# Strided and local attention with a Mish MLP: a new order of local k's transposes and of the strided P·V in the first batch

## The chip, the cores and the metric

The kernel runs on one core of a Trainium2 chip. The metric is the device time of one execution in microseconds (us), as the median of several runs. The engines of the core work side by side, each through its own queue in order: TensorE (PE; its weight loads are listed as PEld), VectorE (DVE), ScalarE (ACT), GpSimd (POOL) and SyncE (SP, here only a queue of DMAs). PE writes its results into PSUM, from where DVE and ACT copy them on.

## The reference, cut to what matters

There are 8 batches, 8 heads, 576 positions and a head dimension of 64. Heads 0 to 3 are local (a query sees the 32 positions up to its own), heads 4 to 7 are strided (a query sees earlier positions with the same remainder modulo 32). The attention's output feeds an MLP on 4608 tokens.

```
scores = scale * np.matmul(q, k.transpose(0, 1, 3, 2))
mask_local = (rel >= 0) & (rel < stride)
mask_strided = (rel >= 0) & (pos[None, :] % stride == pos[:, None] % stride)
scores = np.where(masks[None, :, :, :], scores, -1000000000.0)
attn = np.exp(scores - max); attn = attn / (sum(attn) + 1e-09)
x = matmul(attn, v) as [4608, 512]
h = x @ w_in                      # 512 -> 2048
g = h * np.tanh(softplus(h))      # Mish
out = g @ w_out                   # 2048 -> 512
```

## The kernel before, in words

The work runs in nine token blocks of 512 for the MLP (t = 0 to 8) and eight batches of attention. From batch 1 on, the attention of a batch is spread in small steps between the matmuls of the MLP. Batch 0 has nothing to be spread into: lines 693 to 740 are its attention by itself, written out by hand in the order in which each engine's queue gets it, and the edit is in there. There is no planner; what is emitted first on an engine is done first on it (`manual_schedule`, L649), and semaphores hold an instruction until its inputs are written and the memory that it writes is free.

The stages of batch 0, and the helpers that emit them:

- `t_step(b, kind, which, hp, eng)` (L221) transposes one half (two heads) of q or k on PE into a PSUM tile `tr`, 8 transposes for the strided kind "s" (L229) and 12 for the local kind "l" (L243), and copies it to SBUF on the engine that is named (L180 on ACT, L182 on DVE): `kTs`, `qTs`, `kTl`, `qTl`. The PSUM tiles come from a pool of two buffers (`tile_t`, L114), used in turn, so that the next but one can be written only when the copy out of the first is done.
- `a.bias(kind, i, i_acc)` (L274) writes the mask into one of three accumulators of two banks each (acc0, acc1, acc2), by matmuls of an identity with a constant (L280). `a.qk([(kind, i)], None, ps)` (L287) adds the scores on top (L303) and lets ACT take their exp into `P_s[i]` or `P_l[i]` (L311). Both kinds come in three parts: 12, 12 and 8 matmuls with 864, 864 and 576 columns for "s", and 10, 10 and 4 with 960, 960 and 384 for "l".
- `a.pv2(kind, i, i_acc)` (L350) does P·V for the pair i, i+1 in an accumulator (8 matmuls, L333); DVE then takes the reciprocal of the row sums (L358) and scales the result into `x_s` or `x_l` (L359). Strided pairs 0, 2, 4 and 6 need parts 0, 0 and 1, 1, and 2. Local pairs 0, 2 and 4 need parts 0, 0 and 1, and 1 and 2.
- `unread(n, i_acc)` (L253) issues n matmuls of 512 columns of zeros, whose result nobody reads. They go to a `tr` tile, or to an accumulator if one is named.
- `a.xt(kind, hf)` (L364) transposes the result (L372, L382) and ACT copies it into `xT`, the MLP's input. `mlp1(0, accs)` (L453) then multiplies by `w_in` (L473, 64 matmuls for t = 0) and ACT takes Mish (L483); `mlp2` multiplies by `w_out` (L573), with the attention of batch 1 between its steps.

The loads that matter here are emitted long ahead: `load_early_loc(0)` (L138) issues the local k and q of batch 0 on POOL's queue. `spread_v_str(0, Dv)` is a DVE copy of the strided v. `load_w_out`, `load_qk_str(1)` and the others of L723 to L730 follow behind the part that is changed.

An accumulator is free for its next use when the engine that reads it is done: ACT's exp for scores, DVE's scaling for P·V. In the old order, the three strided parts use acc0, acc1 and acc2, the strided pairs acc0, acc1, acc0, acc0, the local parts acc2, acc1, acc2, and the local pairs acc1, acc0, acc2.

Of the kernel before, what the change touches and what calls it, by code (L numbers as in the profile page):

```python
# [43 lines left out]
def kernel(ctx, tc, q, k, v, moe_w_in, moe_w_out, out):  # L44
# [55 lines left out]
    def acc(i, name):  # L100

        pool = ps_z[0] if i == 2 else ps_a
        return pool.tile([128, 2, 512], F32, tag=f"acc{i}", name=name)
# [10 lines left out]
    def tile_t(name):  # L114
        return ps_t.tile([128, 512], F32, tag="pt", name=name)
# [11 lines left out]
    def by_head(x):  # L127

        return x[0:PL].rearrange("p j h d -> p (j h d)").rearrange("p (h x) -> p h x", h=4)
# [19 lines left out]
    def spread_v_str(b, eng):  # L149
        cast(eng, vs[b % 2][0:PN, :, :, 0:D], vs_raw().rearrange("p h (j d) -> p h j d", d=D))  # L150
# [27 lines left out]
    def cast(eng, out_, in_):  # L178
        if eng is nc.scalar:
            nc.scalar.copy(out_, in_)  # L180
        else:
            eng.tensor_copy(out_, in_)  # L182
# [38 lines left out]
    def t_step(b, kind, which, hp, eng=None):  # L221

        eng = eng or nc.vector
        tr = tile_t("tr")[:].bitcast(BF16)
        if kind == "s":
            src = (qs if which == "q" else ks)[b % 2]
            for u in range(8):
                h, jj = 2 * hp + u // 4, u % 4
                nc.tensor.transpose(  # L229
                    tr[:, PN * u:PN * u + PN],  # L230
                    src[0:PN, h, 128 * jj:128 * jj + 128],
                    ident[0:PN, 0:PN],
                )
            dst = (qTs if which == "q" else kTs)[:, 8 * SU * hp:8 * SU * hp + 8 * SU]
            cast(
                eng, dst.rearrange("c (u n) -> c u n", u=8)[:, :, 0:PN],
                tr[:, 0:S].rearrange("c (u n) -> c u n", u=8),
            )
        else:
            src = by_head((ql if which == "q" else kl)[b % 2])  # L240
            for j in range(CL):
                for e in range(2):
                    nc.tensor.transpose(  # L243
                        tr[64 * e:64 * e + 64, PL * j:PL * j + PL],
                        src[:, 2 * hp + e, D * j:D * j + D], ident[0:PL, 0:PL],
                    )
            dst = qTl[:, hp, :] if which == "q" else kTl[:, hp, 32:32 + S]
            cast(
                eng, dst.rearrange("c (p j) -> c p j", j=CL),
                tr[:, 0:S].rearrange("c (j p) -> c p j", j=CL),  # L250
            )

    def unread(n, i_acc=None):  # L253

        tr = tile_t("un")[:] if i_acc is None else acc(i_acc, "un")[:, 0, :]
        for _ in range(n):
            nc.tensor.matmul(tr, lhsT=zeros[:, 0:128], rhs=zeros[:], start=True, stop=True)
# [391 lines left out]
    with tc.manual_schedule():  # L649
        Po, Dv, Sc = nc.gpsimd, nc.vector, nc.scalar  # L650
# [42 lines left out]
        a = Attn(0)  # L693
# [5 lines left out]
        ps = [a.bias("s", i, i) for i in range(2)]  # L699
# [2 lines left out]
        t_step(0, "s", "q", 1, Dv)  # L702
        unread(2, 2)
        ps.append(a.bias("s", 2, 2))
        for i in range(3):
            a.qk([("s", i)], None, ps[i])
        spread_v_str(0, Dv)
        unread(2)
        a.pv2("s", 0, 0)
        for hp in range(2):  # L710
            t_step(0, "l", "k", hp, Sc)
        a.pv2("s", 2, 1)
        unread(2, 2)
        t_step(0, "l", "q", 0, Sc)
        t_step(0, "l", "q", 1, Dv)
        ps = [a.bias("l", 0, 2)]
        a.pv2("s", 4, 0)
        ps.append(a.bias("l", 1, 1))
        a.qk([("l", 0)], None, ps[0])
        a.qk([("l", 1)], None, ps[1])  # L720
        a.pv2("s", 6, 0)
        a.qk([("l", 2)], None, a.bias("l", 2, 2))
        load_w_out(0, 1)  # L723
        load_qk_str(1)
# [117 lines left out]
```

## Time and profile before

| | us |
|---|---|
| median of 3 runs | 305.48 (305.15 to 305.68) |
| the profiled execution | 304.4 |
| its span, first to last instruction | 302.6 |
| PE busy in the span | 293.1 |
| first strided exp, end of the third | 12.25, 14.45 |
| transposes of local k, of local q (first one's start) | 13.54, 15.03 |
| first local exp, start | 17.53 |
| first local P·V, start | 19.42 |
| dense stretch of the first MLP product, start | 22.77 |
| first transposes of batch 1, start | 35.72 |

The profile is that of one execution; its times are in us from the start of its span. A line of the timeline has the start, the time until the end, engine, line, operation, output and inputs, the shape, how often, and in brackets how long the engine was idle before and what ended this. Matmuls are pipelined: one of 512 columns is shown as taking 0.38, but they follow each other every 0.21 to 0.22. A line of the chain of waits has a start, a length, and what was under way in the chain of work that ended last.

### The profile page before, as it was taken

Reading aid. Unit: us, or ns where it says so; the run is one execution under the profiler, and the core shown is the slowest. Engines: PE = TensorE matmul, PEld = TensorE weight load, DVE = VectorE, ACT = ScalarE, POOL = GpSimd, SP = SyncE. Lnnn points to the kernel's source line nnn. Section 1 sums busy time; section 2 is a strip of 40 time slices with the busy share of each in tenths; the row PEclk is TensorE's granted clock in tenths of the full one; section 3 lists DMA queues with packets and bytes.
Section 4 is the critical chain, followed back from the end, with each engine's and each line's share of the span. In section 5 each row is a group of like instructions: output and inputs, shape, how many; then the busy total and the mean of one; then the engine's idle time right before and its main releaser. Section 6 shows DMA issues by size and latency. Waiting matters only on the chain.

```text
span 302.6 us, 6850 instructions
## 1 busy us (share of the span) xinstructions
PE 293.1 (97%) x2900; PEld 197.9 (65%) x2922; DVE 155.8 (51%) x356; ACT 171.7 (57%) x220; POOL 105.4 (35%) x116
## 2 busy tenths in 40 slices
PE   8889999999999999999999999999999999999995
PEld 3554556546884588458889885478646864684484
DVE  2370166868660857086617662576348544620732
ACT  2568634677655765667456855685467636414620
POOL 8284402324491419240934085206620410000000
PEclk9999999999999999999999999999999999999999
DMA  8999999979999998999979975994590030003003
GB/s 158 186 202 194 194 195 191 187 133 200 242 162 188 284 164 129 117 277 174 114 121 281 169 98 100 280 143 84 67 255 1 3 141 0 2 0 141 0 0 141
DMA packets 103738, 43.25 MB, mean 143 GB/s; under 512 B 86172, under 2 KB 99212, under 8 KB 103708
## 3 DMA queue, kind: packets, MB, share of 16 engines
q1 hardware_dynamic: 86620, 30.05, 55.9%
q0 software_dynamic: 16800, 12.51, 27.9%
q8 instruction: 23, 0.38, 0.6%
q10 hardware_dynamic: 288, 0.25, 0.3%
q14 instruction: 7, 0.06, 0.1%
HBM read 38.38 MB, written 9.44 MB: 158 GB/s over the span
## 4 chain that ended last, share of the span: by engine, by line
PE 89%; DVE 3%; DMA 3%; ACT 2%; issue 1%; POOL 0%; ACTq 0%; POOLq 0%
PE psh L473 32%; PE pso L545 28%; PE psb L473 9%; PE po L333 4%; PE pso L573 4%; PE pso L600 4%; PE ps L303 4%; DMA qs<-in_q_dram 3%; DVE x_l L359 2%; PE trx L372 1%; PE trx L382 1%; ACT Ps L311 1%; DVE osb L524 1%; PE tr L229 1%; PE tr L243 1%
## 5 line engine op out<-in xcount | busy, mean ns | idle before, releaser
L473 PE MATMUL psh<-xT,w_in 128*128 128x512 bf16 (+1 forms) x484 | 100.7, 358 | 0.8
L473 PEld LDWEIGHTS <-w_in 128*128 128x128 bf16 x640 | 61.5, 98 | 58.2 <-issue 0.7
L483 ACT ACTIVATE gT<-psh 128x1024 bf16<-128x1024 f32 x56 | 56.3, 1023 | 45.5 <-PE psh L473 43.1
L497 DVE TENSOR_TENSOR Sg<-gT 128x256 bf16<-128x256 bf16 (+2 forms) x64 | 28.4, 450 | 51.0 <-ACT gT L483 48.9
L317 POOL TENSOR_TENSOR Pl<-Pl,consts_sb 128x960 bf16<-128x960 bf16 (+1 forms) x18 | 29.2, 1632 | 48.5 <-ACT Pl L311 48.5
L545 PEld LDWEIGHTS <-Sg 128*128 128x128 bf16 x448 | 41.9, 98 | 6.3
L545 PE MATMUL pso<-Tw,Sg 128*128 128x256 bf16 x336 | 40.1, 273 | 0.0
L545 PEld LDWEIGHTS <-gT 128*128 128x128 bf16 x336 | 31.3, 98 | 4.6
L182 POOL CAST vl<-vl 128x768 bf16<-128x768 f32 x15 | 13.6, 931 | 59.4 <-DMA vl<-in_v_dram 59.4
L180 ACT COPY xT<-trx 128x576 bf16<-128x576 bf16 x32 | 20.1, 639 | 20.0 <-PE trx L382 14.0
L473 PE MATMUL psb<-xT,w_in 128*128 128x512 bf16 (+1 forms) x141 | 30.1, 355 | 0.2
L180 ACT COPY osb<-pso 128x512 f32<-128x512 f32 (+1 forms) x26 | 14.1, 544 | 26.4 <-PE pso L545 16.1
L545 PE MATMUL pso<-w_out,gT 128*128 128x256 bf16 x224 | 27.8, 273 | 0.0
L311 ACT ACTIVATE Pl<-ps 128x960 bf16<-128x960 f32 (+1 forms) x24 | 19.2, 807 | 11.6 <-PE ps L303 11.4
L524 DVE TENSOR_TENSOR osb<-pso,osb 128x512 f32<-128x512 f32 x21 | 14.5, 692 | 21.4 <-PE pso L545 21.4
L311 ACT ACTIVATE Ps<-ps 72x864 bf16<-72x864 f32 (+1 forms) x24 | 18.5, 803 | 5.3 <-PE ps L303 5.1
L479 ACT ACTIVATE gT<-psb 128x512 bf16<-128x512 f32 x32 | 19.0, 598 | 2.9 <-PE psb L473 2.5
L359 DVE TENSOR_TENSOR x_s<-po,rden 72x512 bf16<-72x512 f32 x28 | 19.2, 686 | 1.0
L497 DVE TENSOR_TENSOR Sg<-Sg,gT 128x256 bf16<-128x256 bf16 (+2 forms) x32 | 16.2, 506 | 1.1
L573 PE MATMUL pso<-w_out,gT 128*128 128x512 bf16 x59 | 15.8, 380 | 0.5 <-issue 0.3
L333 PEld LDWEIGHTS <-Ps 72*128 72x128 bf16 x256 | 12.1, 97 | 5.4 <-DVE Ps L317 1.7
L344 DVE RECIPROCAL rden<-po 96x4 f32<-96x4 f32 (+1 forms) x22 | 3.9, 178 | 22.1 <-PE po L333 22.0
(90 smaller groups left out, 343.4 us busy)
## 6 DMA issues: line engine op xcount, KB each, us to landing
out_dram<-osb SPq DMA_DIRECT2D x16, 512.0 KB, 6.2
vl<-in_v_dram SPq DMA_DIRECT2D x7, 768.0 KB, 6.9
kl<-in_k_dram SPq DMA_DIRECT2D x6, 576.0 KB, 9.9
ql<-in_q_dram SPq DMA_DIRECT2D x6, 576.0 KB, 13.1
qs<-in_q_dram POOLq DMA_DIRECT2D x8, 288.0 KB, 11.0
vsr<-in_v_dram POOLq DMA_DIRECT2D x8, 288.0 KB, 7.4
w_in<-in_moe_w_in_dram POOLq DMA_DIRECT2D x4, 512.0 KB, 9.7
w_out<-in_moe_w_out_dram POOLq DMA_DIRECT2D x4, 512.0 KB, 17.3
```

Source lines behind the costliest of these rows:

```text
L180: nc.scalar.copy(out_, in_)
L311: nc.scalar.activation(pt[0:n, :, 0:nw], ps[0:n, :, o0:o0 + nw], AF.Exp, scale=scale)
L317: meng.tensor_tensor(out=pm, in0=pm, in1=mk[0:n, :].unsqueeze(1).unsqueeze(1).to_broadcast([n, 2, nu, w]), op=ALU.mult,)
L333: nc.tensor.matmul(po[:, h, :], lhsT=pt[0:n, c0:c0 + 128], rhs=rhs, start=True, stop=True,)
L359: nc.vector.tensor_tensor(out=dst.rearrange("p e (h d) -> p e h d", h=4), in0=po[0:m, :, :, 0:D], in1=rden[0:m].unsqueeze(3).to_broadcast( ...
L473: nc.tensor.matmul(ps_u[:, o:o + n], lhsT=w_in[:, cc, fc * 128:(fc + 1) * 128], rhs=xT[:, cc, a:a + n], start=(cc == 2 and (o == 0 or len( ...
L479: nc.scalar.activation(gT[:, g + 8 * u, :], ps_u[:], AF.Mish)
L483: nc.scalar.activation(to, tiles[g][:], AF.Mish)
L497: nc.vector.tensor_tensor(out=out_, in0=in0, in1=in1, op=op)
L524: add = lambda o, p: nc.vector.tensor_tensor(out=o, in0=p, in1=o, op=ALU.add)
L545: nc.tensor.matmul(ps[:, pair, :], lhsT=lhs(c, 128 * pair), rhs=rhs(c), start=(first and pair == 0 and c == 0), stop=(last and c == 7), sk ...
L573: nc.tensor.matmul(p[:, ot % 2, :], lhsT=gT[:, fc, 128 * ot:128 * ot + 128], rhs=w_out[:, fc, :], start=(fc == 0), stop=(fc == 15),)
```

## The change

The edit is in lines 705 to 721, all of it in the order of batch 0's attention.

The transposes of local k, which stood behind the first strided P·V, now stand ahead of the third strided scores. Half 0 is copied by DVE instead of ACT; half 1 stays on ACT, where its copy is now between the second and the third strided exp. Three fillers stand ahead of them instead of two, and the two fillers ahead of local q are gone. The first two strided P·V pairs follow the third strided scores. Both halves of local q are copied by ACT; half 1 was copied by DVE.

The fourth strided P·V pair (pair 6) is moved ahead of the local scores, and goes from acc0 to acc1. The second local part goes from acc1 to acc0, and its bias is emitted behind the first local scores instead of ahead of them.

The amount of attention work stays as it was; one filler of 512 columns is gone in all. No DMA is moved.

```
-        for i in range(3):
+        for i in range(2):
             a.qk([("s", i)], None, ps[i])
         spread_v_str(0, Dv)
-        unread(2)
+        unread(3)
+        t_step(0, "l", "k", 0, Dv)
+        t_step(0, "l", "k", 1, Sc)
+        a.qk([("s", 2)], None, ps[2])
         a.pv2("s", 0, 0)
+        a.pv2("s", 2, 1)
         for hp in range(2):
-            t_step(0, "l", "k", hp, Sc)
-        a.pv2("s", 2, 1)
-        unread(2, 2)
-        t_step(0, "l", "q", 0, Sc)
-        t_step(0, "l", "q", 1, Dv)
+            t_step(0, "l", "q", hp, Sc)
         ps = [a.bias("l", 0, 2)]
         a.pv2("s", 4, 0)
-        ps.append(a.bias("l", 1, 1))
+        a.pv2("s", 6, 1)
         a.qk([("l", 0)], None, ps[0])
-        a.qk([("l", 1)], None, ps[1])
-        a.pv2("s", 6, 0)
+        a.qk([("l", 1)], None, a.bias("l", 1, 0))
         a.qk([("l", 2)], None, a.bias("l", 2, 2))
```

## The prediction

> **What bounds the kernel now.** I read the page first: TensorE (PE) is busy for 97% of the span, and the chain of work that ended last is PE for 89%. So a gain must come from a place where that chain leaves PE. From 22.77 us on it hardly does; before that it does. The second view was therefore the chain in order of time for the first 24 us (columns: start us, length us, what; L311 is exp, L180/L182 are copies, L243 the transposes of local q and k, L303 scores, L333 P·V, L359 the scaling of the output, L372 transposes of the output, L473 the first MLP product):
>
> ```profile
> 12.25 2.20 ACT Ps L311 x3
> 14.45 1.07 ACT kTl L180 x2
> ...
> 15.57 0.45 PE tr L243 x12
> 16.01 0.51 PE ps L280 x2
> ...
> 17.53 1.84 ACT Pl L311 x2
> 19.42 0.45 PE po L333 x8
> ...
> 20.13 0.69 DVE x_l L359
> ...
> 21.80 0.70 DVE x_l L359
> 22.55 0.39 PE trx L372 x5
> 22.93 1.08 PE psh L473 x5
> ```
>
> Three ScalarE (ACT) exps run back to back, then ACT copies both transposed halves of local k, and only the release of those PSUM tiles lets PE transpose local q. After that come local scores, two exps, P·V and three scalings on VectorE (DVE) in a row; PE then starts its dense work. The third view is the timeline: what the first local P·V waits for, and what follows.
>
> ```profile
> 16.05 0.76 DVE L182 COPY qTl<-tr 128x576 bf16<-128x576 bf16 x1 [0.49 <-PE tr L243]
> 18.56 0.33 PE L280 MATMUL ps<-consts_sb 128*128 128x192 bf16 x2 [0.35 <-ACT Pl L311]
> 19.42 0.43 PE L333 MATMUL po<-vl,Pl 128*128 128x65 bf16 x8 [0.35 <-ACT Pl L311]
> 22.77 13.12 PE L473 MATMUL psh<-xT,w_in 128*128 128x512 bf16 x59
> ```
>
> That P·V (windows 0 and 1) reads only the first local exp, over since 18.50. It waits to 19.42 because its accumulator, acc1, holds the second local scores until the second exp ends (19.36). In the next view (DMA issues; last column: us from issue to landing) are the two loads that the change reaches for earlier, and the one with least margin later. They are issued at 3.61, 4.29 and 25.86, so they land at 12.8, 14.5 and 45.3.
>
> ```profile
> kl<-in_k_dram POOLq DMA_DIRECT2D x1, 288.0 KB, 9.2
> ql<-in_q_dram POOLq DMA_DIRECT2D x1, 288.0 KB, 10.2
> w_out<-in_moe_w_out_dram POOLq DMA_DIRECT2D x1, 512.0 KB, 19.4
> ```
>
> **The change, step by step.** I lay the new order on the old durations. Starts that nothing changes: the first strided scores at 11.84, exp s0 12.25 to 13.13, exp s1 13.03 to 13.91 (ACT exps of 864 columns follow each other every 0.78, local ones of 960 every 0.87, copies every 0.54).
>
> 1. *Local k.* 24 score matmuls are issued by 12.35 (32 took until 12.47), three fillers take 3 x 0.215 = 0.64 (five took 1.24, the last of them 0.38), so the k transposes start at 13.03 instead of 13.54. The load landed at 12.8; no wait. Twelve transposes end 0.45 after they start. DVE copies half 0 (0.76, the row of qTl above) from 13.50 to 14.26. Half 1 ends at 13.76 on PE, and ACT takes it at 13.81, behind exp s1, until 14.45.
> 2. *Third strided scores.* Eight matmuls at 13.67, exp s2 on ACT at 14.35 to 14.99, against 13.81 to 14.45. This 0.54 of delay is a cost, but only P·V of strides 6 and 7 reads that exp.
> 3. *Strided P·V.* The first pair goes from 13.20 to 13.90, the second from 14.18 to 14.17. On DVE the scaling (0.20 + 0.69, one pair every 0.84) now stands behind the copy of kTl: x_s of the four pairs end at 15.27, 16.10, 16.94 and 17.77 (before: 14.58, 15.56, 17.73, 19.17).
> 4. *Local q.* Its tile is free at 14.26, but the load lands only at 14.5: start 14.55 instead of 15.03. This wait on a DMA is new; behind it PE has nothing else to do. Halves end at 15.00 and 15.27; both copies are on ACT now, 15.02 to 15.66 and 15.56 to 16.20 (the DVE copy ended at 16.81).
> 5. *The rest of the strided P·V and the bias.* Bias of local part 0 at 15.20 (needs exp s2, 14.99), pair 4 at 15.61, pair 6 at 16.17 (its acc1 is free when x_s of pair 2 ends, 16.10). Local scores 0 at 16.50, 0.30 behind the q copy for the PE queue in front of it. Exp l0: 16.92 to 17.89, before 17.53 to 18.50.
> 6. *Local part 1 in acc0.* Its bias waits for x_s of pair 4 (16.94), a new wait: 17.00 plus 0.51 to the scores plus 0.42 to their end. Exp l1 is 17.93 to 18.90 (before 18.40 to 19.36). Part 2: bias at 17.95, scores 18.20, exp 18.80 to 19.30.
> 7. *First local P·V.* acc1 is now free at 17.77, so it goes when PE reaches it: 18.37 instead of 19.42. Three scalings end 19.75, 20.58, 21.42, where the last ended at 22.50. The second P·V needs exp l1 (18.90) and the third exp l2 (19.30); both are done before DVE gets to them. ACT's xT copies end at 19.84 and 20.38, and PE's four MLP matmuls end at 21.08, so neither is later than DVE.
> 8. *Dense work* follows the last transposes: 21.42 + 0.28 = 21.70 instead of 22.77. **Gain 1.07 us.**
>
> Each of these starts is good to some 0.1; the gap between unlike matmuls is the softest (0.07 to 0.12 in the rows, some ten of them, of which old and new have nearly as many).
>
> Is the gain kept? No DMA-issuing instruction is moved, or moved past another on SP's or POOL's queue: all of them stand behind the edit, and what they wait for is a DMA or data that is early. What PE would meet sooner: w_in's third and fourth pieces land at 23.05 and 25.6 and are first used 28 and 44 matmuls behind 21.70, at 27.7 and 31.1; batch 1's q for the strided heads lands at 33.0, used at 34.9; w_out's third piece, at 45.3, is first used at 47.24, then 46.17. The narrowest margin is this 0.9. From 58 us on the view of waits shows PE waiting for no load, and the DMA transposes for batch 2 land by 68, used at 73.
>
> **Sum.** The profiled execution took 304.4 us (span 302.6, 1.8 around it): 304.4 - 1.07 = 303.3. The median of the runs shown is 1.08 above that execution, so I give 305.48 - 1.07 = 304.4. Two unknowns have ends on both sides. If the first local P·V has to wait for exp l1 all the same (its accumulator or a coarser count of ACT's work), it goes at 18.96, 0.59 later: gain 0.48. If DVE fits the first scaling before the copy of kTl, and q needn't wait for its load, scores l0 come some 0.3 sooner: gain 1.4. I take 1.07, since every wait in it has a row that names its releaser.
>
> **A cost that the sum holds at nothing: PE's speed.** The change issues one filler fewer in net and drops two that ran just before the q transposes; PE will stand idle 0.1 to 0.5 us at a time between 14.4 and 18. That PE does not always run at one pace, the start shows, in the groups of matmuls between 2 and 3 us, and between 6.6 and 7.5 (busy us, mean ns of one): the same 512 columns took 634 ns until some 4.6 us, though the granted clock reads 1.00 there, and 379 later. The row of 18 to 20 us (length, PE busy, PEld, DVE, ACT, POOL busy, granted clock, DMA share, GB/s) has gaps like those to come, with PE busy for 65%:
>
> ```profile
> L257 PE MATMUL un<-zeros 128*128 128x512 bf16 x4 | 1.9, 634 | 0.0
> ...
> L257 PE MATMUL un<-zeros 128*128 128x512 bf16 x3 | 0.8, 379 | 0.0
> ```
>
> ```profile
> 18.00:20.00 2.00, 1.30 (x31) 0.91 (x28) 1.00 (x3) 1.75 (x3) 2.00 (x3) 1.00 1.17 189
> ```
>
> The dense matmuls behind that row have a mean of 379 too, so those gaps cost nothing, and I go by it. The Trainium skill, TensorE: Matmul & The Clock Gate, speaks against dropping fillers: "A second HAM failure mode: psum-queue depth-cycling" says that frequent small idles between groups of matmuls can make the clock swing between half and full, and Part 1 there gives a window of 3.4 us. By that rule one window at half speed would cost an estimated 1.7 us, and the sum would be about 306.1.
>
> **Rivals.**
> - *A wait takes the place of the old one* (20%). Either acc1 or exp l1 still holds the first local P·V, or the DVE queue (copy of kTl, then four scalings) delays bias l1 more than I have. For it: DVE's x_s of pair 0 is 0.69 later than before, and acc0 and acc1 each wait for such a scaling. Against it: the local P·V has 0.6 us of margin on x_s of pair 6 (17.77 against 18.37); only pair 6 and bias l1 are bound by such a scaling, and that is in the sum. Gain 0.0 to 0.6, taken at 0.48: 305.0.
> - *The gain is made and then hidden* (7%): w_out's third piece, or a load whose landing moves with PE, takes it back. Against it: 0.9 of margin. It would need a landing after 47; then nearly no change, 305.4.
> - *Slower: the matmuls fall back to 634 ns* (10%). The place is the head of the dense stretch. There a matmul would be 634 - 379 = 0.255 us longer; the gain of 1.07 is used up by four such, and the kernel is over 0.2% slower from seven on (1.68). A spell as long as the one at the start (1.2 to some 4.6, 3.4 us, eight at a spacing of some 0.43) costs up to 8 x 0.255 = 2.0, and by the spacings (0.43 - 0.215) 1.7: net +0.6 to +0.9, taken at +0.7, 306.2. For it: fewer fillers. Against it: the mean of 379 behind the old gaps.
>
> **Chances.** Forecast, gain 0.7 to 1.4: 60%; more than that, 3%; the three rivals as above, 37%. What a measurement of this kernel can tell from no change is 0.2%, 0.61 us: faster beyond that takes the forecast, the 3% and a part of the first rival (0.68), within it the rest of that rival and the second (0.22), slower the 634 ns (0.10). The range runs from the large gain (304.0) over the partial gain to the hidden one (305.5); the 634 ns are left out.
>
> **What would show it.** Right: transposes of kl near 13.0, of ql near 14.5 behind their load, exp l0 at 16.9, the first local P·V at 18.4 with no wait for an exp, the last x_l ending at 21.4, the dense stretch from 21.7, and every later landmark (36.24, 58.55, 74.24) earlier by the same 1.07. Wrong: a P·V that waits for "ACT Pl", a bias l1 later than 17.2, a later landmark that has moved by less, or dense matmuls above 379 ns.

## The result

The changed kernel took 304.15 us (303.31 to 304.44, 8 runs) beside 305.21 (304.57 to 305.68, 8 runs) of the one before: a ratio of 0.9962 with an interval of 0.9948 to 0.9976. That is 1.06 us less, and by the interval 0.7 to 1.6 us; on record are 304.4 and a gain of 1.07. The execution that was profiled took 303.47, its span is 301.7.

The profile after, first the chain of waits for the first 24 us (start, length, what), as it was read in the prediction:

```profile
12.36 0.75 PE un L257 x3
13.12 0.63 PE tr L243 x24
...
14.62 0.69 DVE x_s L359
...
15.45 0.70 DVE x_s L359
...
16.19 0.42 PE po L333 x8
16.61 0.34 PE ps L303 x10
...
16.98 0.97 ACT Pl L311
...
17.97 1.35 ACT Pl L311 x2
19.32 1.08 ACT xT L180 x2
...
21.57 0.39 PE trx L372 x5
21.96 2.16 PE psh L473 x10
```

The two copies of local k are gone from the chain, and so is the wait for the tiles of local q. In their place stand the transposes of k and the scalings (x_s) of the first two strided pairs, which pair 6 waits for. Behind the exps the chain now runs over ScalarE's copies of xT. Then come the lines of the timeline for the first local P·V, the last transposes of the local output (here their weight loads, PEld) and the dense stretch:

```profile
18.45 0.43 PE L333 MATMUL po<-vl,Pl 128*128 128x65 bf16 x8
21.57 0.24 PEld L372 LDWEIGHTS <-x_l 96*128 96x128 bf16 x5 [0.16 <-DVE x_l L359]
21.79 13.12 PE L473 MATMUL psh<-xT,w_in 128*128 128x512 bf16 x59
```

The P·V has no bracket any more: it waits for no exp. The last five transposes still wait for VectorE's last scaling, which ends at 21.52; the seven ahead of them are issued by 21.35, so ScalarE's copies of xT, though the chain runs over them, are a little early. The dense stretch is as long as it was and starts 0.98 us earlier. The landmarks behind it are earlier by as much, 57.41 instead of 58.39 and 88.67 instead of 89.65; the end of the last matmul comes 0.93 earlier, 298.29 instead of 299.22.

| event, us | before | predicted | after |
|---|---|---|---|
| strided q transposes, start | 10.32 | 10.32 | 10.29 |
| local k transposes, start | 13.54 | 13.03 | 13.05 |
| exp s2, start | 13.81 | 14.35 | 14.33 |
| last x_s, end | 19.17 | 17.77 | 17.81 |
| local q transposes, start | 15.03 | 14.55 | 14.51 |
| exp l0, start | 17.53 | 16.92 | 16.98 |
| bias of local part 1 | 16.60 | 17.00 | 17.03 |
| first local P·V | 19.42 | 18.37 | 18.45 |
| last x_l, end | 22.50 | 21.42 | 21.52 |
| dense stretch, start | 22.77 | 21.70 | 21.79 |

### The profile page after: what moved, and what is told of

It reads as the page before. It is cut to its first block, busy times and chain, and to the rows that moved or that the text cites. A ratio compares the mean times of both kernels' runs of the same rounds, so it can differ in the third digit from the quotient of the medians.

```text
span 301.7 us, 6848 instructions
## 1 busy us (share of the span) xinstructions
PE 293.5 (97%) x2900; PEld 198.4 (66%) x2921; DVE 156.4 (52%) x356; ACT 171.8 (57%) x220; POOL 108.1 (36%) x116
## 4 chain that ended last, share of the span: by engine, by line
PE 92%; DVE 4%; ACT 2%; issue 1%; ACTq 0%
PE psh L473 32%; PE pso L545 27%; PE psb L473 9%; PE po L333 4%; PE pso L573 4%; PE pso L600 4%; PE ps L303 4%; PE un L257 3%; PE trx L372 2%; PE trx L382 1%; DVE x_l L359 1%; DVE osb L524 1%; PE tr L229 1%; ACT Pl L311 1%; PE tr L243 1%
## 5 line engine op out<-in xcount | busy, mean ns | idle before, releaser
L497 DVE TENSOR_TENSOR Sg<-gT 128x256 bf16<-128x256 bf16 (+2 forms) x64 | 29.8, 471 | 50.9 <-ACT gT L483 48.7
L180 ACT COPY xT<-trx 128x576 bf16<-128x576 bf16 x32 | 20.2, 641 | 19.5 <-PE trx L382 13.6
```

The lines of the kernel that those rows point to most:

```text
L497: nc.vector.tensor_tensor(out=out_, in0=in0, in1=in1, op=op)
```

## The experiments

Two questions were open. Which part of the edit earns the time: the k copies between the exps, or the exchange of accumulators that frees the first local P·V? And does the gain arrive at the end? The runs lie within 1 us of each other, so each is read in two ways: by the ratio of many runs, and in the profile by a stretch that holds the edit and little else, from the start of the strided q transposes (set ahead of the edit, by their load or by the first fillers) to the start of the dense stretch. It is 12.45 us before (22.77 - 10.32) and 11.50 after (21.79 - 10.29): 0.95 us. A second profile of the changed kernel, below, has 11.51.

**Only the second half of the edit.**

```
         a.pv2("s", 4, 0)
-        ps.append(a.bias("l", 1, 1))
+        a.pv2("s", 6, 1)
         a.qk([("l", 0)], None, ps[0])
-        a.qk([("l", 1)], None, ps[1])
-        a.pv2("s", 6, 0)
+        a.qk([("l", 1)], None, a.bias("l", 1, 0))
```

> The old order of local k and q and of the first two strided pairs, with only the second part of the edit: pair 6 ahead of the local scores in acc1, local part 1 in acc0 with its bias behind the first scores. By the sum of the prediction: scores l0 no longer stand behind two biases, exp l0 starts at 17.36 instead of 17.53; bias l1 waits for x_s of pair 4 (17.73), exp l1 ends at 19.69, later than before; but the first local P·V no longer waits for it and goes at 19.0, last x_l ends at 22.05, dense stretch at 22.3: gain 0.45 us. A rival in which all the gain comes from k between the exps expects 0.0 here; one in which all of it comes from the accumulators expects 1.0.

Measured: 304.50 us beside 304.80 of before, ratio 0.9987 (0.9977 to 0.9997). The stretch is 12.10 (22.55 - 10.45), 0.35 shorter where 0.45 was expected. In the timeline of its profile the bias of part 1 is late, as expected:

```profile
17.91 0.58 PE L280 MATMUL ps<-consts_sb 128*128 128x480 bf16 x2 [0.45 <-DVE x_s L359]
```

PE stands idle for 0.45 us until the scaling of pair 4 ends, because that pair still comes behind the old, late copy of q. The first local P·V is free of exp l1, but goes only at 19.21.

**Only the first half**: the changed kernel with the old lines of that second diff.

> The new order of local k and q, with the old second part: local part 1 in acc1 with its bias ahead of the first local scores, pair 6 behind them in acc0. By the sum: q copies end at 16.20, bias l1 waits for x_s of pair 2 (16.10), exp l0 starts at 17.1, exp l1 ends at 18.93, and the first local P·V waits for it in acc1 and goes at 19.0; last x_l at 22.04, dense stretch at 22.3: gain 0.46 us. The rival in which all comes from k between the exps expects 1.0, the rival of the accumulators alone 0.0.

Measured: 304.52 us beside 304.80, ratio 0.9990 (0.9980 to 1.0001), a gain that this comparison can't tell from none. The stretch is 12.09 (22.68 - 10.59), 0.36 shorter where 0.46 was expected. Exp l0 stands 0.35 nearer to the q transposes (6.86 instead of 7.21), but the first local P·V goes at 19.34 behind exp l1, in acc1. So neither half is the change: 0.35 and 0.36 leave 0.24 of the 0.95 that only both together give, since each half runs into the wait that the other removes.

**The wait itself put back.** The changed kernel, with local pairs 0 and 2 exchanged between acc0 and acc1.

```
-        accs = (1, 0, 2)
+        accs = (0, 1, 2)
...
-        a.pv2("l", 0, 1)
+        a.pv2("l", 0, 0)
...
-        a.pv2("l", 2, 0)
+        a.pv2("l", 2, 1)
```

> The changed kernel, with local pairs 0 and 2 exchanged between acc0 and acc1 (and the first MLP groups with them), so that the first local P·V shares its accumulator with local part 1 again and must wait for exp l1. By the sum: P·V at 18.9 instead of 18.45, the dense stretch 0.4 to 0.5 us later than in the changed kernel, about 22.25, half of the gain lost. The rival, that the scalings of the strided pairs on VectorE or the ScalarE copies of xT set the dense stretch and not the release of acc1, expects no change against the changed kernel (21.8).

The line of its timeline that answers to 18.45 above:

```profile
19.04 0.43 PE L333 MATMUL po<-vl,Pl 128*128 128x65 bf16 x8 [0.48 <-ACT Pl L311]
```

The wait is back, for ScalarE's second exp, and the stretch is 12.05 (22.39 - 10.34): 0.55 of the 0.95 are lost, so the release of the accumulator does set the dense stretch. The time, 304.88 beside 304.80 (ratio 1.0002, 0.9993 to 1.0012), lost all of the gain, for a second reason that is not the question here: with the accumulators of the MLP exchanged too, the next block's first matmuls wait 0.6 us for a copy of ScalarE (psh behind osb in the view of waits).

**Without the fillers ahead of k.** The line `unread(3)` is taken out.

> The changed kernel without the three fillers ahead of the k transposes. By the sum: the transposes wait for the load of kl (12.8) and start at 12.85 instead of 13.05, the scalings of the strided pairs move up by as much, pair 6 and the local scores by 0.15 to 0.2: dense stretch at 21.6, 0.15 us earlier than in the changed kernel. The rival that fillers are needed for PE's pace expects dense matmuls of more than 379 ns behind 21 us and up to 1.7 us lost.

Measured: 303.79 beside 304.80, ratio 0.9959 (0.9947 to 0.9971). Two lines of the timeline show that PE now waits for both loads:

```profile
12.68 0.70 PE L243 MATMUL tr<-consts_sb,kl 96*64 96x96 bf16 x24 [0.38 <-DMA kl<-in_k_dram]
14.49 0.70 PE L243 MATMUL tr<-consts_sb,ql 96*64 96x96 bf16 x24 [0.22 <-DMA ql<-in_q_dram]
```

The k transposes stand 2.46 behind the strided q transposes instead of 2.76, yet those of q no earlier than with the fillers: that load is the bound, as step 4 had it. The dense stretch starts at 21.60, the stretch is 11.38, 0.12 shorter, with matmuls at 379 ns as ever. In this place the three fillers aren't needed: without them the clock stays, and so does the pace.

**Without any filler behind the first sixteen**: `unread(3, 2)`, `unread(5, 2)` and `unread(2, 2)` are taken out as well.

> The changed kernel without any filler behind the first sixteen (13 fewer matmuls of 512 columns). By the sum PE waits for loads more often up to 14.6, its pace stays, and the time is that of the kernel without the three fillers ahead of k, 0.4% below before. The rival of the prediction, that fillers hold the pace, expects matmuls of 512 columns at 634 instead of 379 ns for some 3.4 us and 1.7 us or more lost: slower than before.

Measured: 306.58 beside 305.06, ratio 1.0050 (1.0031 to 1.0068). My sum was wrong for this one, and the rival's mechanism is real. The columns of the rows of stretches are as in the prediction: length, PE busy, and so on, with the granted clock third from the end.

```profile
8.00:12.00 4.00, 2.64 (x54) 1.75 (x54) 0.63 (x2) 1.56 (x4) 1.59 (x2) 1.00 1.38 188
12.00:16.00 4.00, 3.06 (x65) 2.70 (x64) 2.13 (x5) 2.74 (x4) 0.00 (x0) 0.62 1.63 188
16.00:20.00 4.00, 3.93 (x50) 2.24 (x48) 2.53 (x7) 2.15 (x3) 3.74 (x6) 0.50 1.21 196
20.00:24.00 4.00, 4.00 (x58) 3.09 (x58) 1.68 (x4) 2.53 (x4) 4.00 (x6) 0.50 1.24 205
24.00:28.00 4.00, 3.78 (x23) 2.15 (x22) 0.91 (x3) 2.18 (x3) 1.62 (x3) 0.68 1.20 188
28.00:32.00 4.00, 4.00 (x20) 1.83 (x19) 0.00 (x0) 3.14 (x4) 2.50 (x3) 1.00 1.25 191
```

A mean of 0.62 over four us is half speed from about 13.0 on, and 0.68 is half speed until about 26.6; the first transposes of batch 1 are at 39.27 instead of 34.75. This profile is of the slowest of the ten runs. Nine of them have a mean granted clock of 0.976 to 0.983 over the span and take 306.01 us or more; the tenth kept 1.00 and took 304.81. So it is the clock that costs the time, and it doesn't fall every time. The ten fillers between the strided stages keep it up without the three ahead of k (0.999 to 1.000 in the six runs of the kernel above); which of the ten are needed, and whether the three alone would do, was not tried. The Trainium skill, TensorE: Matmul & The Clock Gate, Part 1, has the halved clock after an idle window of about 3.4 us. No such window is to be seen here: from the first filler to the fall PE's longest gap is 1.14 us, in front of the strided q transposes. The length of the spell, 13.6 us, is near four of the page's windows, though the row of 16 to 20 us shows PE busy for 3.93 of 4.

**Both halves of k on ScalarE**: `t_step(0, "l", "k", 0, Sc)` in the changed kernel.

> The changed kernel with both halves of local k copied by ScalarE between the exps, as the old one did behind them; VectorE copies none. By the sum: exp s2 and both q copies are 0.4 to 0.5 later, q ends at 16.6 instead of 16.20, scores l0 at 16.7 instead of 16.5, dense stretch 0.15 us later, 11.65 us behind the q transposes of the strided heads. The rival that VectorE's scalings are what binds, and its copy of k the cost of the change, expects 0.2 to 0.5 us earlier.

Measured: 304.27 beside 305.06, ratio 0.9977 (0.9965 to 0.9989). The stretch is 11.73 (22.38 - 10.65), 0.23 longer than with VectorE's copy. So VectorE's copy is no hidden cost but a quarter of the gain in the profile. In the times the two can't be told apart: the unaltered kernel beside it, on the same chip, had 0.9975.

**The changed kernel again, and one that fills the last gap.** The second puts `g1s[1]()` between the two local `a.xt` calls.

> The changed kernel once more, unaltered, as the measure for the runs beside it. Expected: 0.35 to 0.4% faster than before; from the q transposes of the strided heads to the dense stretch 11.5 us (12.45 in the old profile). If a cast on GpSimd late in the first 80 us lies over VectorE's masks of batch 2 in one execution and not in another, the profile of this run shows the second MLP block (57.4 to 88.7 in the first profile) either at 31.26 or some 0.4 longer; the rival that such a difference belongs to the kernel expects 31.26 again.

> The changed kernel with the last transposes of the local output behind the MLP matmuls of group 1 instead of ahead of them, so that PE works while VectorE does the last scaling. If that scaling is what the dense stretch waits for, as in the prediction, PE's gap in front of it (0.2 us) goes and batch 1's first transposes come 0.2 us earlier against the q transposes of the strided heads than in the changed kernel (24.46); if ScalarE's copies of xT are the bound, no change.

Measured: the changed kernel 304.29 beside 305.06, ratio 0.9975 (0.9963 to 0.9987), less than in the first comparison (0.9962) although its stretch is 11.51 (21.65 - 10.14). Its second block is 31.26 long, so it did not show the difference that I looked for. With the gap filled, 303.79, ratio 0.9961 (0.9946 to 0.9977); batch 1's first transposes come 24.36 (35.14 - 10.78) behind the strided q transposes instead of 24.46. That is half of what was expected. This profile does show the longer block: 31.73 from 57.81 to 89.54, where batch 2's attention starts. The lines of its timeline there:

```profile
73.33 1.81 POOL L182 CAST vl<-vl 128x768 bf16<-128x768 f32 x2 [8.27 <-DMA vl<-in_v_dram]
73.66 0.80 DVE L497 TENSOR_TENSOR Sg<-gT,Sg 128x256 bf16<-128x256 bf16 x1
74.37 0.91 DVE L497 TENSOR_TENSOR Sg<-gT 128x256 bf16<-128x256 bf16 x1
75.80 1.11 DVE L317 TENSOR_TENSOR Ps<-Ps,consts_sb 72x864 bf16<-72x864 bf16 x2
76.45 0.42 PE L333 MATMUL po<-vs,Ps 72*128 72x65 bf16 x8 [0.44 <-DVE Ps L317]
```

GpSimd (POOL) casts v as soon as its load lands (73.21). While it does, VectorE's additions take 0.80 and 0.91 us instead of 0.29 (the length of the same shape at 71.93), its masks behind them come late, and PE waits 0.44 us for a mask. In the first profile of the changed kernel the cast came at 71.58, over earlier additions, and PE lost no time to it. Of the profiles without the next edit, four have a second block of 31.63 to 31.73 us (first half only, no fillers ahead of k, k on ScalarE, and this one; casts from 73.33 to 74.58), three have 31.26 (before, the second half only, and the first of the changed kernel; 71.58 to 72.52), and so have the changed kernel's second profile (73.27) and the one without fillers (74.54, with all of PE's work later). The exchanged pairs are left out, since the wait for ScalarE stands at the head of that block. So a late cast alone is not enough: at 73.27 it met only one addition (0.91 us), and at 73.67 and 74.58, without the fillers ahead of k and with k on ScalarE, it met a mask itself (1.10 and 1.15 us instead of 0.60).

**The cast moved out of the way**, in both kernels: on SP's queue the load of v goes ahead of the DMA transposes of local k and q.

```
         def load_rest2():
-            transpose_by_dma(2)
+            transpose_str(2)
             load_v_loc(2)
+            transpose_loc(2)
...
-                    at[10] += [lambda: transpose_by_dma(t + 2), lambda: load_v_loc(t + 2)]
+                    at[10] += [lambda: transpose_str(t + 2), lambda: load_v_loc(t + 2), lambda: transpose_loc(t + 2)]
```

`transpose_by_dma` is cut in two for this, `transpose_str` for the strided heads and `transpose_loc` for the local ones.

> The old kernel, with the load of local v of the next batches put on SP's queue ahead of the DMA transposes of local k and q instead of behind them, so that GpSimd's cast of v comes some 5 us earlier, away from VectorE's masks of the strided heads. If the casts that lie over these masks cost 0.3 to 0.45 us per block in some executions, the second and third MLP block are 31.26 and 31.23 long here in each profile, and the median is 0.1 to 0.4 us under the old one's. The rival, that these differences come from the loads themselves, expects blocks of 31.6 or more here too.

> The changed kernel with the same earlier load and cast of local v. If the collisions hide a part of the change's gain, blocks of 31.26 and 31.23, a median near 303.4, the lower of the two levels that the changed kernel's times fall on (303.3 to 303.5 and 304.1 to 304.4), and 0.95 us under the old kernel with the same edit, which is what batch 0's attention gains in the profiles. If the collisions are no part of it, 304.2 as before.

Measured on the same chip, beside 304.78 of the kernel before: the old kernel with this edit 304.44, ratio 0.9988 (0.9979 to 0.9996), its 11 runs from 304.19 to 304.71; the changed one 303.47, ratio 0.9965 (0.9953 to 0.9977), with seven of its ten runs from 303.28 to 303.54. The other three, 303.94 to 304.63, are still above that, so not all of the spread comes from these casts. Between the two medians lie 0.97 us, near the 0.95 of the profiles; between the two ratios lie 0.0023, which is 0.70 us. From the timeline of the changed one (its lines are numbered 6 higher):

```profile
68.27 1.82 POOL L182 CAST vl<-vl 128x768 bf16<-128x768 f32 x2 [3.61 <-DMA vl<-in_v_dram]
73.25 0.29 DVE L503 TENSOR_TENSOR Sg<-gT,Sg 128x256 bf16<-128x256 bf16 x1
74.79 0.60 DVE L323 TENSOR_TENSOR Ps<-Ps,consts_sb 72x864 bf16<-72x864 bf16 x1 [0.45 <-ACT Ps L317]
```

The cast is done by 70.1, the addition takes 0.29 and the mask 0.60, and it is VectorE that waits for ScalarE. The second and third blocks are 31.26 and 31.23 long in this profile, and 31.27 and 31.23 in that of the old kernel with the edit. With the load earlier and the casts gone from the masks, all of the difference is gone from these blocks.

**All three edits together**: no fillers ahead of k, group 1 between the local transposes, v's load earlier.

> The changed kernel with three edits: no fillers ahead of the k transposes, the last transposes of the local output behind the MLP matmuls of group 1, and the earlier load of local v. Expected 0.1 us from each of the first two, and no casts over masks: near 303.2, 0.6% under before. A rival in which an earlier first block runs into w_out's third piece or into later collisions expects no more than the changed kernel's gain.

Measured: 303.48 beside 304.78, ratio 0.9962 (0.9948 to 0.9977), not better than the changed kernel with the load of v alone (303.47 beside the same runs). In its profile the gap of the local transposes is closed, and batch 1's first transposes stand 24.15 behind the strided q transposes instead of 24.46:

```profile
21.13 0.42 PE L378 MATMUL trx<-consts_sb,x_l 96*128 96x96 bf16 x6
21.39 1.03 PE L479 MATMUL psh<-xT,w_in 128*128 128x512 bf16 x4
22.25 0.42 PE L378 MATMUL trx<-consts_sb,x_l 96*128 96x96 bf16 x6
```

Without the fillers ahead of k alone that distance is 24.33 (34.55 - 10.22), so the filled gap brings 0.18 here, near the 0.2 expected. The three tenths of the profile are not shown in the time of the five runs (303.19 to 304.26).

## Why the prediction was right

Steps 1 to 8 hold one by one; no start in the table is off by more than 0.10 us, and the errors add up to 0.09 at the end, so that the gain is 0.98 in this pair of profiles. That the medians differ by 1.06, all but the 1.07 on record, is partly luck: the interval runs from 0.7 to 1.6 us, and the second comparison gave 0.77 (305.06 - 304.29). The wait on the load of q (step 4) is there, though one sees it only without the fillers (0.22 us); the waits of pair 6 and of bias l1 on VectorE are there; and what pays is step 7, the accumulator that the first local P·V no longer shares with local part 1. The exchanged pairs show that this accumulator is worth 0.55 of the 0.95, and the half edits that the second half brings only 0.35 without steps 1 to 4 in front of it.

The first rival did not come about, but its price was right: put back, the wait costs 0.55, with 0.59 on record. The rival of the matmuls' pace did not come about either, and the matmuls of the dense stretch stay at 379 ns; it is right about fillers as such. I had it from the wrong place, though. Where the clock fell, PE had been busy for only 2.64 of the 4 us from 8 to 12, waiting for loads; the gaps of 0.1 to 0.5 us from 14 to 18, which I had feared, cost nothing. The price was wrong too: one window and 1.7 us were on record, and the spell lasted 13.6 us and put batch 1's first transposes 4.5 us further behind the strided q transposes (28.97 instead of 24.46) in that profile, the slowest run; between the medians lie 2.3 us (306.58 beside 304.29).

The weak step is "Is the gain kept?". I asked which loads PE would meet sooner, found 0.9 us of margin, and gave 7% to a load that hides the gain. I did not ask which loads another engine acts on. GpSimd's cast of v starts with a landing and not with PE's work, and VectorE's masks of batches 2 and 3 stand on PE's path; where a cast meets these masks, or the last additions ahead of them, 0.3 to 0.5 us can be lost per block. That such meetings lengthen a block, and that moving the cast removes them, the profiles show. What they cost either kernel on the mean is about as much as the runs can tell apart: the earlier load took 0.1% from the old kernel (ratio 0.9988), and the changed one has 0.9965 with it and 0.9962 and 0.9975 without. That the change makes the meetings more frequent, by moving the masks 1 us ahead of a landing that does not move, is argued and not shown. With the casts out of the way the change is worth 0.70 to 0.97 us, by ratios or medians, which is no more than without. Why the landing differs between executions (casts from 71.58 to 74.58) was not tried; most of the difference is there when the load is issued on SP's queue (65.56 in the first profile of the changed kernel, 68.46 with k on ScalarE).

## What to carry to other kernels

A wait can be held by the buffer and not by the data: ask for each waiting matmul what its output's last reader is, and exchange buffers before making anything faster. Take an order apart before crediting a part of it: here each half was worth a little over a third, because each ended in the wait that the other removed. And where a gain moves one engine against a transfer, look at what a third engine does when that transfer lands.

## What the runs showed of the hardware that I had not expected

- GpSimd's casts and VectorE's instructions on two SBUF operands hold each other up in these profiles: additions of 0.29 us became 0.80 and 0.91 under two casts that took 1.81 together. The Trainium skill, SBUF — State Buffer, "Who interferes with whom", says that a VectorE instruction with two SBUF inputs contends with a GpSimd instruction that reads SBUF, and that such contention is an exclusive lock. The lines above agree: the additions are longer by 0.5 and 0.6, and the second ends at 75.28, just behind the casts (75.14).
- The pace of the first sixteen fillers differs between executions of the same instructions: they took from 5.01 to 6.45 us in the profiles. In the first profile of the changed kernel they took long enough to be the bound themselves:

```profile
1.20 6.27 PE L257 MATMUL un<-zeros 128*128 128x512 bf16 x16 [1.20 <-DVE zeros L664]
```

  The load of the strided q had landed at 10.06 (issued at 2.21), but PE came to it at 10.29, behind the fillers; in the old profile the load landed at 10.27 and PE had waited for it.
- Without the fillers PE was busy for 2.64 of the 4 us from 8 to 12; in nine of ten runs the clock fell. In the profiled one it stayed at half for about 13.6 us, although PE was busy for 4.00 of the 4 us from 20 to 24.
